# Two transfers change their queue and gain a wait: gate weights on GpSimd's queue, and a hold before the first accumulating transfer

## The chip, the cores and the metric

The kernel runs on one core of a Trainium2 chip. A core has five engines that work side by side and meet at semaphores: TensorE (matrix products, PE in the profile; its weight loads are PEld), VectorE (DVE), ScalarE (ACT), GpSimd (POOL) and SyncE (SP), which here only issues transfers. Sixteen DMA engines carry out the transfers that SP, ScalarE and GpSimd issue; the profile calls SP's queue q1, ScalarE's q10 and GpSimd's q0. The metric is the device time of one execution in microseconds (us).

## The reference

A block of a transformer over 2048 tokens of width 512, in bf16, reduced here to what is computed:

```python
# x: (1, 2048, 512); 32 heads of 16; window of 8 keys, 2 apart
qkv = layernorm(x) @ wqkv
q, k, v = split(qkv)
logits[s, w] = (q[s] . k[s - 2*w]) * 16 ** -0.5      # -1e9 where s - 2*w < 0
o[s] = sum over w of softmax(logits[s])[w] * v[s - 2*w]
h = x + o @ wo
gate, up = layernorm(h) @ W_gate, layernorm(h) @ W_up   # width 1376
out = h + (relu(gate) * up) @ W_down
```

## The kernel before, in words

**Chunks.** The 2048 tokens are handled in four chunks of 512, each in four blocks of 128. For each chunk the kernel normalizes x (`layernorm`), turns the normalized blocks so that the width lies on the partitions, multiplies by the q, k and v weights, and forms the window attention on VectorE: products of q with k shifted by 0 to 14 tokens (L637 in chunk 0, L620 in the others), sums over a head by matmuls with a 0/1 matrix (L628), exponentials, a broadcast of each head's weight over its 16 rows by DMA (L756, eight issues of SP for a chunk), and products with shifted v (L803 in chunk 0, L788 in the others). These products fill a tile `mt` of eight slices of 512 tokens, one tile for each quarter `t` of the width, and the eight slices are added up.

**The sum over eight slices.** In chunks 0, 1 and 2 (`DACC`) the first halving, slices 4 to 7 onto 0 to 3, is done by a DMA of GpSimd's queue that adds to its destination (L831, `f_da`, the steps `ta0` to `ta3`). VectorE does the other two halvings (L791) and the scaling in chunk 0 (L795), which writes the attention's output `OT`, the input of the projection with wo (L867). At the end of chunk 0's attention two tiny copies of GpSimd (L849, L850, the step `lg`) write into the up and down weight tiles; SP's loads of these weights come after them. In the hand-written order GpSimd issues chunk 0's transfers in the order of quarters 1, 3, 2, 0, and VectorE's products and sums follow the same order of quarters.

**Turning the blocks.** Most blocks are turned by TensorE (L531). For some halves of chunks (`DMAT`), both halves of chunk 3's norm of x among them, SP issues a DMA that transposes (L520), one for each block of 128 tokens. All four write one tile `dst`, which is `[128, 4, 512]`; block `j` goes to its columns from `128*j`.

**Setup.** `setup()` issues the first loads. SP loads x of chunk 1, the v weights (L338), x of chunks 2 and 3 (L341), wo (L343) and then the gate weights in two halves (`f_load`, L311). Some loads are held back by a tiny copy of GpSimd: it writes one element of the load's destination and reads one of a tensor that must have arrived first (L334, L337, L339), so that the load, which overwrites the element, has to come after it. The gate weights come without such a copy, behind wo on SP's queue.

**Order.** Every step of the four chunks is an `Op` with an engine, a planned duration, the steps it depends on and buffers. `Plan.order()` runs through them on a model of the engines. The list `RANK` gives each step, by its number, its place among the steps of its engine, so each engine's order is fixed by hand; the model's start times settle in which order the steps of different engines are written out, and which buffer of a set each step takes. The waits themselves come from the data: an instruction waits for the ones that last wrote what it reads. The steps of the four transposes of chunk 3 have the numbers 588, 592, 590 and 594 for blocks 0, 2, 1 and 3 in the order in which SP runs them.

Of the kernel before, what the change touches and what calls it, by code (L numbers as in the profile page):

```python
# [8 lines left out]
P = 128  # L9
BF16 = mybir.dt.bfloat16  # L10
# [82 lines left out]
class Plan:  # L93
# [9 lines left out]
    def add(self, key, *a, **k):  # L103
        op = Op(*a, **k)
        op.key = key
        op.seq = len(self.ops)
        if RANK:
            op.prio = RANK[op.seq]
        self.ops.append(op)
        for b in set(op.take) | set(op.use):  # L110
            b.left += 1
        return op
# [90 lines left out]
def kernel(  # L203
# [11 lines left out]
    nc = tc.nc  # L215
# [32 lines left out]
    sb = ctx.enter_context(tc.tile_pool(name="sb", bufs=1))  # L248
# [9 lines left out]
    same = sb.tile([P, P], BF16, name="same")  # L258
    mask = sb.tile([P, 2, PADL], BF16, name="mask")
    eps_t = sb.tile([P, 1], F32, name="eps_t")  # L260
    warm = sb.tile([P, P], BF16, name="warm")
    ci = sb.tile([P, 1], I32, name="ci")
    tmp = sb.tile([P, 3], I32, name="tmp")
# [4 lines left out]
    wv_sb = sb.tile([P, NT, D], BF16, name="wv_sb")  # L268
# [33 lines left out]
    def f_load(n, i):  # L302
        if n == "d":
            lo, hi = (0, 5) if i == 0 else (5, NFF)
            nc.sync.dma_start(
                wd_sb[:, lo:hi, :], B_W_down[lo * P:hi * P, :].rearrange("(ft p) n -> p ft n", p=P))
            if FTAIL and i:
                nc.sync.dma_start(wd_sb[:FTAIL, NFF, :], B_W_down[NFF * P:F, :])
        else:
            w = (B_W_gate if n == "g" else B_W_up).rearrange("(dt p) f -> p dt f", p=P)  # L310
            nc.sync.dma_start(wgu_sb[:, 2 * i:2 * i + 2, int(n == "u"), :], w[:, 2 * i:2 * i + 2, :])  # L311

    def setup():

        w3_r = A_wqkv.rearrange("(dt p) f -> p dt f", p=P)
        for i in range(2):
            for n, q in enumerate((nc.sync, nc.scalar)):
                j = 2 * i + n
                q.dma_start(x_sm[:, j:j + 1, :], x_rows[:, j:j + 1, :])
                q.dma_start(wqk_sb[:, j:j + 1, :], w3_r[:, j:j + 1, 0:2 * D])  # L320
        nc.scalar.preload_act_table_set("natural_log_exp_and_others")
        V.memset(warm[:], 0.0)  # L322
        make_identity(nc, identity[:])
        nc.gpsimd.memset(eps_t[:], EPS)
        nc.gpsimd.iota(ci[:], pattern=[[0, 1]], base=0, channel_multiplier=1)
        nc.gpsimd.iota(sel_i[:], pattern=[[1, H]], base=0, channel_multiplier=0)
        nc.gpsimd.iota(sp_i[:], pattern=[[1, H], [0, DQ]], base=0, channel_multiplier=0)
        nc.gpsimd.iota(sm_i, pattern=[[0, 4], [1, H]], base=0, channel_multiplier=0)
        nc.gpsimd.iota(mk_i[:], pattern=[[1, PADL]], base=0, channel_multiplier=0)
        nc.gpsimd.memset(kT[:, :, 0:PADL], 0.0)  # L330
        nc.gpsimd.memset(vT[:, :, 0:PADL], 0.0)


        nc.gpsimd.tensor_copy(out=x_sm[0:1, BPC:2 * BPC, 0:1], in_=wqk_sb[0:1, 0, 0:BPC])  # L334
        for j in range(BPC, 2 * BPC):
            nc.sync.dma_start(x_sm[:, j:j + 1, :], x_rows[:, j:j + 1, :])
        nc.gpsimd.tensor_copy(out=wv_sb[0:1, 0, 0:1], in_=wqk_sb[0:1, 3, 0:1])  # L337
        nc.sync.dma_start(wv_sb[:], w3_r[:, :, 2 * D:3 * D])  # L338
        nc.gpsimd.tensor_copy(out=x_sm[0:1, 2 * BPC, 0:1], in_=x_sm[0:1, 2 * BPC - 1, 0:1])  # L339
        for tk in range(2, NCK):  # L340
            nc.sync.dma_start(x_sm[:, tk * BPC:(tk + 1) * BPC, :], x_rows[:, tk * BPC:(tk + 1) * BPC, :])  # L341

        nc.sync.dma_start(wo_sb[:], A_wo.rearrange("(p t) f -> p t f", t=NT))  # L343
        for n in "gud":
            for i in range(2):
                if n not in LATE:
                    f_load(n, i)


        for n, (op, by) in enumerate(((ALU.arith_shift_right, 2), (ALU.bitwise_and, H - 1),  # L350
                                      (ALU.arith_shift_right, 5))):
            V.tensor_scalar(out=tmp[:, n:n + 1], in0=ci[:], scalar1=by, scalar2=None, op0=op)
        V.tensor_copy(out=cf[:, 0:3], in_=tmp[:])
        V.tensor_scalar(out=cf[:, 2:3], in0=cf[:, 2:3], scalar1=1.0 * DIL, scalar2=None, op0=ALU.mult)
        V.tensor_scalar(out=cf[:, 3:4], in0=cf[:, 2:3], scalar1=4.0 * DIL, scalar2=None, op0=ALU.add)
        V.tensor_scalar(out=sel[:], in0=sel_i[:], scalar1=cf[:, 0:1], scalar2=None, op0=ALU.is_equal)
        V.tensor_scalar(out=spread[:], in0=sp_i[:], scalar1=cf[:, 1:2], scalar2=None, op0=ALU.is_equal)
        V.tensor_scalar(out=same[:], in0=sm_i, scalar1=cf[:, 1:2], scalar2=None, op0=ALU.is_equal)
        for hf in range(2):
            V.tensor_scalar(out=mask[:, hf, :], in0=mk_i[:], scalar1=cf[:, 2 + hf:3 + hf],  # L360
                            scalar2=None, op0=ALU.is_ge)
# [11 lines left out]
    PRS, MUH = (0,), (0,)  # L373
    TDD, TDL = 1.3, 1.5
    NWARM, NFILL = 56, (13, 10, 0)
    NHALF = 8
    XT = (3.47, 3.64, 5.45, 5.97, 7.8, 8.2, 8.65, 9.1, 14.8, 16.5)
    WT = (7.75, 7.75, 5.0, 12.5, 18.0, 24.95, 21.4, 28.8)
# [54 lines left out]
    def layernorm(tk, src, dst_slots, pr, groups, on_act, residual=None):  # L433
# [6 lines left out]
        evs = []  # L440
        for grp in groups:
# [72 lines left out]
            for j0 in range(lo, hi, step):  # L514
                if (ln, tk, j0) in DMAT:
                    for j in range(j0, min(j0 + step, hi)):
                        xn, a = norm(j)

                        def f_td(j=j, xn=xn):
                            nc.sync.dma_start_transpose(out=dst.t[:, :, j * P:(j + 1) * P], in_=xn.t[:])  # L520

                        evs.append(add((ln + "td" + gk, tk), "SP", TDD, f_td, [a], pr, take=[dst], use=[xn], lat=0.5, dq=(0.1, 0.64)))
                    continue
                tp, ds, xs = Buf(tp_s), [], []
                for j in range(j0, min(j0 + step, hi)):
                    xn, a = norm(j)

                    def f_tp(j=j, j0=j0, xn=xn, tp=tp):
                        for t in range(NT):
                            o = t * 2 * P + (j - j0) * P  # L530
                            nc.tensor.transpose(tp.t[:].bitcast(BF16)[:, o:o + P],  # L531
                                                xn.t[:, t * P:(t + 1) * P], identity[:])

                    ds.append(add((ln + "tp" + gk, tk), "PE", 4 * TP, f_tp, [a], pr, take=[tp], use=[xn], lat=PEL))
                    if tk == 0 and not residual and j < 2:
                        fill(ds[-1], NFILL[j])
                n = len(ds)

                tev = not residual and tk == 0 and j0 == 1

                def f_ev(j0=j0, n=n, tp=tp, tev=tev):
                    i = tp.t[:].bitcast(BF16).rearrange("p (t c) -> p t c", t=NT)[:, :, 0:n * P]
                    o = dst.t[:, :, j0 * P:(j0 + n) * P]
                    if tev:
                        V.tensor_copy(out=o, in_=i)
                    else:
                        nc.scalar.copy(out=o, in_=i)  # L547

                evs.append(add((ln + ("tv" if tev else "te") + gk, tk), "DVE" if tev else "ACT", 0.36 if tev else (A10 if n == 2 else A5), f_ev, ds, pr, take=[dst], use=[tp], lat=AL))
# [5 lines left out]
    for tk in range(NCK):  # L555
# [224 lines left out]
        for t in range(NT):  # L780
# [46 lines left out]
            for n, du in ((4, D20), (2, D10), (1, D2)):  # L827
                f = lambda n=n, mt=mt, f=f_a: f(n, mt)
                if n == 4 and (tk, t) in DACC:
                    def f_da(mt=mt):  # L830
                        nc.gpsimd.dma_start(mt.t[:, 0:4, :], mt.t[:, 4:8, :], accum_op=ALU.add)  # L831

                    ms = [m] = [add(("ta%d" % t, tk), "POOL", 1.0, f_da, ms, tpr, use=[mt], lat=1.1, dq=(0.75, 2.74))]
                    continue
                if n == 2 and (tk, t) in DAC2:
                    def f_db(mt=mt):
                        nc.gpsimd.dma_start(mt.t[:, 0:2, :], mt.t[:, 2:4, :], accum_op=ALU.add)

                    ms = [m] = [add(("tb%d" % t, tk), "POOL", 0.95, f_db, ms, tpr, use=[mt], lat=1.1, dq=(0.75, 1.37))]
                    continue  # L840
                if n == 1 and tk in EARLY:
                    oev[t] = add(("tree%d" % t, tk), "DVE", du, f_al, ms, tpr, take=[OT], use=[mt], lat=DL)
                else:
                    ms = [m] = [add(("tree%d" % t, tk), "DVE", du, f, ms, tpr, use=[mt], lat=0.11)]
# [232 lines left out]
```

## Time and profile before

| | us |
|---|---|
| median of 3 runs | 194.53 (194.43 to 194.96) |
| the profiled execution | 194.99 |
| its span, first to last instruction | 192.9 |
| TensorE busy in the span | 189.1 |
| VectorE busy | 150.8 |
| ScalarE busy | 115.7 |
| GpSimd busy | 17.3 |

The profile is of one execution; its granted TensorE clock is 1.00 throughout. Its time differs from its span by what lies before the first and after the last instruction. In the page's groups a line such as `L831 POOL DMA_DIRECT2D big<-big x12 | 10.9, 933` names the line of the kernel, the engine, the operation, destination and source by the program's names, the count, the busy time in us and the mean duration in ns. In the order of time a row begins with start and length in us. For DMA issues the length is that of issuing; the time to landing is given apart.

### The profile page before, as it was taken

Reading aid. Unit: us, or ns where it says so; the run is one execution under the profiler, and the core shown is the slowest. Engines: PE = TensorE matmul, PEld = TensorE weight load, DVE = VectorE, ACT = ScalarE, POOL = GpSimd, SP = SyncE. Lnnn points to the kernel's source line nnn. Section 1 sums busy time; section 2 is a strip of 40 time slices with the busy share of each in tenths; the row PEclk is TensorE's granted clock in tenths of the full one; section 3 lists DMA queues with packets and bytes.
Section 4 is the critical chain, followed back from the end, with each engine's and each line's share of the span. In section 5 each row is a group of like instructions: output and inputs, shape, how many; then the busy total and the mean of one; then the engine's idle time right before and its main releaser. Section 6 shows DMA issues by size and latency. Waiting matters only on the chain.

```text
span 192.9 us, 3122 instructions
## 1 busy us (share of the span) xinstructions
PE 189.1 (98%) x1149; PEld 100.5 (52%) x1149; DVE 150.8 (78%) x243; ACT 115.7 (60%) x241; POOL 17.3 (9%) x35
## 2 busy tenths in 40 slices
PE   7999999999999999999999999999999999999994
PEld 7997455555445434644554434444644444464543
DVE  6789999999999999898999979699976534021414
ACT  3479988858897936965265579622647900465500
POOL 3100002311000013100055000003000000000000
PEclk9999999999999999999999999999999999999999
DMA  5789385993914659974269924646001054002033
GB/s 201 240 273 379 104 200 108 198 193 52 370 47 110 123 167 195 189 170 106 43 124 198 195 44 105 169 82 109 3 0 27 1 107 164 30 0 54 0 126 95
DMA packets 25214, 24.61 MB, mean 128 GB/s; under 512 B 11408, under 2 KB 21488, under 8 KB 25200
## 3 DMA queue, kind: packets, MB, share of 16 engines
q1 hardware_dynamic: 22176, 16.26, 30.4%
q0 software_dynamic: 2304, 7.34, 20.6%
q10 hardware_dynamic: 720, 0.82, 1.3%
q8 instruction: 9, 0.15, 0.3%
q14 instruction: 5, 0.04, 0.1%
HBM read 8.42 MB, written 2.10 MB: 55 GB/s over the span
## 4 chain that ended last, share of the span: by engine, by line
PE 98%; DVE 0%; issue 0%
PE bank L940 36%; PE bank L572 22%; PE bank L990 20%; PE bank L867 7%; PE bank L628 4%; PE bank L421 3%; PE bank L907 3%; PE bank L531 2%; PE bank L429 1%; PE bank L713 0%; PE bank L870 0%; DVE row L1003 0%; DVE warm L322 0%
## 5 line engine op out<-in xcount | busy, mean ns | idle before, releaser
L940 PE MATMUL bank<-quad,wgu_sb 128*128 128x512 bf16 x320 | 72.0, 379 | 0.0
L940 PEld LDWEIGHTS <-wgu_sb 128*128 128x128 bf16 x320 | 31.0, 98 | 36.9 <-issue 1.3
L947 ACT ACTIVATE gr<-bank 128x512 bf16<-128x512 f32 x40 | 23.6, 599 | 26.8 <-PE bank L940 24.8
L990 PE MATMUL bank<-wd_sb,gT 128*128 128x512 bf16 (+3 forms) x198 | 39.2, 355 | 0.0
L572 PE MATMUL bank<-quad,wqk_sb 128*128 128x512 bf16 (+1 forms) x160 | 29.8, 336 | 0.1
L990 PEld LDWEIGHTS <-gT 128*128 128x128 bf16 (+1 forms) x198 | 18.4, 98 | 19.4
L620 DVE TENSOR_TENSOR big<-quad,kT 128x4096 bf16<-128x4096 bf16 x12 | 27.2, 2286 | 0.0
L788 DVE TENSOR_TENSOR big<-big,vT 128x4096 bf16<-128x4096 bf16 x12 | 26.9, 2288 | 0.2 <-issue 0.2
L968 DVE TENSOR_TENSOR gT<-gr,up_sb 128x1024 bf16<-128x1024 bf16 x20 | 13.5, 690 | 16.8 <-ACT gr L947 9.9
L944 ACT CAST up_sb<-bank 128x512 bf16<-128x512 f32 x40 | 22.7, 591 | 4.0 <-issue 1.3
L572 PEld LDWEIGHTS <-wqk_sb 128*128 128x128 bf16 x160 | 17.5, 113 | 9.6 <-DMA x_sm<-in_A_x_dram 0.2
L831 POOL DMA_DIRECT2D big<-big x12 | 10.9, 933 | 74.2 <-DVE big L788 45.3
L791 DVE TENSOR_TENSOR big<-big 128x1024 bf16<-128x1024 bf16 (+2 forms) x24 | 16.8, 730 | 0.1
L572 PE MATMUL bank<-quad,wv_sb 128*128 128x512 bf16 x64 | 15.7, 380 | 0.0
L867 PE MATMUL bank<-wo_sb,quad 128*128 128x512 bf16 x64 | 15.1, 379 | 0.0
L547 ACT COPY quad<-bank 128x1024 bf16<-128x1024 bf16 (+1 forms) x10 | 8.6, 889 | 8.5 <-PE bank L531 8.5
L1003 DVE TENSOR_TENSOR row<-x_sm,bank 128x512 bf16<-128x512 bf16 (+2 forms) x10 | 5.6, 582 | 9.8 <-PE bank L990 9.8
L456 ACT ACTIVATE row<-x_sm,mv 128x512 bf16<-128x512 bf16 x12 | 8.6, 717 | 6.8 <-DVE mv L448 6.5
L467 DVE BATCH_NORM_STATS2 st<-x_sm 128x6 f32<-128x512 bf16 x16 | 10.3, 676 | 0.6 <-DMA x_sm<-in_A_x_dram 0.5
L878 DVE SCALAR_TENSOR_TENSOR x_sm<-x_sm,bank 128x512 bf16<-128x512 bf16 x12 | 8.2, 687 | 3.2 <-PE bank L867 3.0
L580 ACT CAST vT<-bank 128x512 bf16<-128x512 f32 x16 | 9.1, 604 | 2.4 <-PE bank L572 2.4
L572 PEld LDWEIGHTS <-wv_sb 128*128 128x128 bf16 x64 | 7.0, 114 | 6.6 <-issue 1.3
(78 smaller groups left out, 175.0 us busy)
## 6 DMA issues: line engine op xcount, KB each, us to landing
big<-big POOLq DMA_DIRECT2D x12, 512.0 KB, 5.8
big<-ex SPq DMA_DIRECT2D x32, 128.0 KB, 2.7
wgu_sb<-in_B_W_gate_dram SPq DMA_DIRECT2D x2, 688.0 KB, 9.1
wgu_sb<-in_B_W_up_dram SPq DMA_DIRECT2D x2, 688.0 KB, 6.1
wd_sb<-in_B_W_down_dram SPq DMA_DIRECT2D x2, 640.0 KB, 4.6
x_sm<-in_A_x_dram SPq DMA_DIRECT2D x2, 512.0 KB, 6.2
x_sm<-up_sb POOLq DMA_DIRECT2D x4, 256.0 KB, 4.5
out_dram<-x_sm SPq DMA_DIRECT2D x4, 256.0 KB, 2.5
```

Source lines behind the costliest of these rows:

```text
L467: V.bn_stats(out=st.t[:], in_=x_sm[:, tk * BPC + j, :])
L572: nc.tensor.matmul(mm.t[:, lo:hi], lhsT=wv_sb[:, dt, t:D:NT] if c == 2 else wqk_sb[:, dt, c * D + t:(c + 1) * D:NT], rhs=xnT.t[:, dt, lo:h ...
L620: V.tensor_tensor(out=pb.t[:].rearrange("p (t w) s -> p t w s", t=2), in0=q4, in1=k4, op=ALU.mult)
L788: V.tensor_tensor(out=mt.t[:], in0=ab.t[:], in1=v8, op=ALU.mult)
L791: V.tensor_tensor(out=mt.t[:, 0:n, :], in0=mt.t[:, 0:n, :], in1=mt.t[:, n:2 * n, :], op=ALU.add)
L831: nc.gpsimd.dma_start(mt.t[:, 0:4, :], mt.t[:, 4:8, :], accum_op=ALU.add)
L867: nc.tensor.matmul(od.t[:], lhsT=OT.t[:, t, j * P:(j + 1) * P], rhs=wo_sb[:, t, :], start=(t == 0), stop=(t == NT - 1 and tk not in RPE))
L940: nc.tensor.matmul(mm.t[:fs, lo:hi], lhsT=wgu_sb[:, dt, g, ft * P: ft * P + fs], rhs=hnT.t[:, dt, lo:hi], start=(dt == 0), stop=(dt == NT ...
L944: nc.scalar.copy(out=ub.t[:fs, i, :], in_=um.t[:fs, :])
L947: nc.scalar.activation(out=gr.t[:fs, i, :], in_=gm.t[:fs, :], func=ACT.Relu)
L968: V.tensor_tensor(out=gt.t[:fs, 0:n, :], in0=gr.t[:fs, 0:n, :], in1=ub.t[:fs, 0:n, :], op=ALU.mult)
L990: nc.tensor.matmul(od.t[:, c0:c1], lhsT=gts[ft].t[:fs, ft % 2, j * P:(j + 1) * P], rhs=wd_sb[:fs, ft, c0:c1], start=(ft == 0), stop=(ft == ...
```

## The change

Two edits. The gate weights' two loads are issued by GpSimd's queue in place of SP's, after a new copy on GpSimd that writes the first element of each gate row group and reads the v weights' tile. And a new copy on GpSimd, ahead of chunk 0's first accumulating transfer, reads one element of block 2 of chunk 3's transposed norm into a new tile `held` that nothing else reads. In the plan all four transfers of chunk 0 get that transpose as a further dependency.

```diff
+    held = sb.tile([P, 1], BF16, name="held")
...
             w = (B_W_gate if n == "g" else B_W_up).rearrange("(dt p) f -> p dt f", p=P)
-            nc.sync.dma_start(wgu_sb[:, 2 * i:2 * i + 2, int(n == "u"), :], w[:, 2 * i:2 * i + 2, :])
+            (nc.gpsimd if n == "g" else nc.sync).dma_start(wgu_sb[:, 2 * i:2 * i + 2, int(n == "u"), :], w[:, 2 * i:2 * i + 2, :])
...
+        nc.gpsimd.tensor_copy(out=wgu_sb[0:1, :, 0, 0:1], in_=wv_sb[0:1, :, 0:1])
         nc.sync.dma_start(wo_sb[:], A_wo.rearrange("(p t) f -> p t f", t=NT))
...
+    HOLD = ("x", 3, 2)
+    holding, turned = [], {}
...
                         evs.append(add((ln + "td" + gk, tk), "SP", TDD, f_td, [a], pr, take=[dst], use=[xn], lat=0.5, dq=(0.1, 0.64)))
+                        if (ln, tk, j) == HOLD:
+                            turned[HOLD] = dst
+                            for h in holding:
+                                h.deps.append(evs[-1])
...
-                    def f_da(mt=mt):
+                    def f_da(mt=mt, tk=tk):
+                        if tk == 0 and HOLD in turned:
+                            nc.gpsimd.tensor_copy(out=held[0:1, 0:1], in_=turned.pop(HOLD).t[0:1, 0, HOLD[2] * P:HOLD[2] * P + 1])
                         nc.gpsimd.dma_start(mt.t[:, 0:4, :], mt.t[:, 4:8, :], accum_op=ALU.add)
...
+                    if tk == 0:
+                        holding.append(m)
```

## The prediction

> **What bounds the kernel now.** I read the page's busy times first, then the chain of work that ended last, in order of time.
>
> ```profile
> span 192.9 us, 3122 instructions
> PE 189.1 (98%) x1149; PEld 100.5 (52%) x1149; DVE 150.8 (78%) x243; ACT 115.7 (60%) x241; POOL 17.3 (9%) x35
> ```
>
> ```profile
> 0.99 6.08 PE bank L421 x56
> ...
> 21.89 0.98 PE bank L628 x16
> ...
> 34.46 13.81 PE bank L572 x64
> 48.27 0.86 PE bank L867 x4
> ...
> 62.68 0.98 PE bank L572 x4
> 63.67 1.73 PE bank L940 x8
> ...
> 190.20 0.02 issue
> ```
>
> The reader is to see that TensorE is never left waiting from 0.99 to 190.20 us: each piece starts where the last ended. 64 matmuls of 512 columns take 13.81 us, 0.216 each, and four take 0.86, so the pieces run at one pace; a few are longer by 0.1 (0.98 at 62.68). Hence two things. A transfer that comes sooner has nothing to win but these crumbs, well under half a microsecond together. And a VectorE step that comes late costs TensorE whatever exceeds the slack at that place, and TensorE has no idle time later in which to get it back. So the question is only whether either edit makes somebody late.
>
> **SP loses two gate loads.** SP in order of time; the columns are start, length, engine, line, operation.
>
> ```profile
> 9.70 0.93 SPq L341 DMA_DIRECT2D x_sm<-in_A_x_dram  x2
> ...
> 11.22 1.76 SPq L311 DMA_DIRECT2D wgu_sb<-in_B_W_gate_dram  x2
> 21.93 5.28 SPq L756 DMA_DIRECT2D big<-ex  x8
> 27.31 5.25 SPq L520 DMA_TRANSPOSE quad<-row  x4
> ```
>
> The two issues occupy SP from 11.22 to 12.98. SP's next work, the broadcasts of chunk 0 (L756), starts at 21.93 because the masked exponentials are done then. Nine idle microseconds lie between: the 1.76 us freed are worth 0.
>
> **GpSimd gains a copy and two loads.**
>
> ```profile
> wv_sb<-in_A_wqkv_dram SPq DMA_DIRECT2D x1, 512.0 KB, 4.1
> 9.50 0.18 POOL L339 COPY x_sm<-x_sm 1x1 bf16<-1x1 bf16 x1 [1.23 <-DMA x_sm<-in_A_x_dram]
> 32.14 1.01 POOL L831 DMA_DIRECT2D big<-big  x1 [22.46 <-DVE row L502]
> 38.72 0.86 POOL L831 DMA_DIRECT2D big<-big  x1 [1.41 <-DVE big L803]
> 45.92 0.70 POOL L850 COPY wd_sb<-big 1x11 bf16<-1x11 bf16 x1
> ```
>
> The v weights are issued at 8.3 and land 4.1 us later, at 12.4. The copy is like the one of L339 (0.18), each load like the issues of L831 (0.86 to 1.01). The first of these was released when its product ended at 31.54 (below) and starts at 32.14, so 0.6 goes from release to issue. Thus 12.4 + 0.2 + 0.6 + 2 x 1.0 = 15.2 us, and GpSimd would have stood idle until 32.1 (22.46 us of idle time in that row): behind the copy that waits for the v weights there are only the two loads and, from 31.5 on, chunk 0's transfers. On GpSimd the cost is 0.
>
> The bytes are the same, on another queue. Three stretches, whose last two columns are the busy share of the DMA engines and GB/s, give the time:
>
> ```profile
> 14.60:21.00 6.40, 6.40 (x63) 4.48 (x62) 6.40 (x7) 6.40 (x12) 0.00 (x0) 1.00 0.86 332
> 21.80:26.00 4.20, 4.20 (x32) 2.07 (x32) 4.20 (x15) 3.27 (x8) 0.00 (x0) 1.00 0.54 122
> 36.00:44.50 8.50, 8.50 (x41) 4.47 (x40) 8.40 (x8) 6.14 (x12) 1.72 (x2) 1.00 1.02 192
> ```
>
> GpSimd's first gate bytes should flow about 1.4 us after its issue at 13.2 (the first accumulating transfer is issued at 32.14, and the engines fill up from about 33.5), at 14.6. From there 6.4 x 332 = 2120 KB are left, 1410 of them gate, 710 of them x and wo; at a full share the pace is 332 / 0.86 = 386 GB/s. They end near 20.5, as before. The lower pace is that of the accumulating transfers, 192 GB/s: 1410 KB take 7.3 us, and with the 710 KB before them at 386 (1.8) the end is 23.7. I take 20.5 to 21.5: plain loads are nearer to the loads of the first row than to additions.
>
> Who needs what, and when:
>
> ```profile
> x_sm<-in_A_x_dram SPq DMA_DIRECT2D x1, 512.0 KB, 6.6
> big<-ex SPq DMA_DIRECT2D x2, 128.0 KB, 2.9
> 21.82 1.28 DVE L467 BATCH_NORM_STATS2 st<-x_sm 128x6 f32<-128x512 bf16 x2
> 27.71 2.36 DVE L803 TENSOR_TENSOR big<-big,vT 128x2048 bf16<-128x2048 bf16 x2
> ```
>
> Chunk 3's x, the second of the two at 9.70, is issued at 10.1 and lands 6.6 later, at 16.7; VectorE reads it first at 21.82, 5.1 us on. Even if gate took the engines first, at the pace of loads, x would be in with 520 KB of wo still to come, 1.4 us ahead of the end: 19 to 20. wo is used at 48.27 and gate at 63.67. The first four broadcasts are issued by 24.0 and land 2.9 later, near 26.9, for a product at 27.71: margin 0.8. With the engines free of gate at 21.5 they are not late, and at 23.7, before the fourth is issued, hardly. Term: 0.
>
> **The hold.** In the hand-written order the four transposes of chunk 3 have ranks 152 (block 0), 161 (block 2), 168 (block 1) and 176 (block 3), so block 2, which the new copy reads, is second on SP.
>
> ```profile
> 28.74 1.21 SPq L520 DMA_TRANSPOSE quad<-row  x1
> DMA to landing us min/median/max: 2.4/2.5/2.7
> 30.32 1.22 DVE L803 TENSOR_TENSOR big<-big,vT 128x2048 bf16<-128x2048 bf16 x1
> 31.34 1.22 SPq L520 DMA_TRANSPOSE quad<-row  x1
> big<-big POOLq DMA_DIRECT2D x1, 512.0 KB, 6.4
> 45.85 0.68 DVE L791 TENSOR_TENSOR big<-big 128x1024 bf16<-128x1024 bf16 x1
> 47.12 0.75 DVE L795 TENSOR_TENSOR quad<-big,rec 128x512 bf16<-128x512 bf16 x2
> ```
>
> The second transpose is issued at 28.74 and lands at 31.1 to 31.4. The copy then takes between 0.18 (as L339) and 0.70 (as L850, eleven elements beside a busy VectorE): it ends between 31.3 and 32.1. The first accumulating transfer can't go before its product ends anyway: 30.32 + 1.22 = 31.54. So the wait hides behind that product and only the copy may show: 0 to 0.6 us, of which I take 0.1, since one element is nearer to L339.
>
> What is queued behind it on GpSimd: the four transfers of chunk 0, then the two copies at 45.66 and 45.92 that release SP's up and down loads. VectorE waits for the four sums. The transfers fill the engines without a pause (share 1.02 from 36 to 44.5), so a late first one makes the last one as late. That one is issued at 38.72, lands 6.4 later at 45.1, and its sum is read at 45.85: slack 0.75. So 0.1 is hidden, and even 0.6. Beyond 0.75 nothing is: the last product ends at 47.87, and TensorE starts the output projection (L867) right at the end of its matmuls (chain, 48.27). From there VectorE's delay is TensorE's.
>
> The planner's times do not move either: the block's planned landing lies ahead of the planned start of the first transfer, as it does in the trace, so order and buffers stay.
>
> **Sum.** SP 0, GpSimd 0, the transfers' new place 0, the hold 0. The profiled execution took 194.99 us, 192.9 in its span and 2.1 around it; the median of the runs shown is 194.53, 0.46 lower. With nothing to add, the forecast is that median: 194.5. A measurement of this kernel can tell about 0.3%, 0.58 us, from no change.
>
> **Rivals.**
>
> *GpSimd and VectorE get in each other's way (slower).* While GpSimd writes the descriptors of the gate loads, from 13.2 to 15.2, VectorE runs the products of L637 without a pause until 21.8, and the score matmuls (L628) start right with their end, so there is no slack at all. If VectorE waited for both issues, 2 x 0.86 = 1.7 us would reach TensorE: 196.2. If instead the descriptors waited for VectorE, gate would flow from 21.8, 1410 KB at 386 GB/s for 3.7 us, into the broadcasts; 1.9 of that fits into idle engine time (from 21.8 to 26 the share is 0.54 of 4.2 us), 1.8 delays them, 0.8 is their margin: 1.0 us, 195.5. It decides once a product of L637 is lengthened, or gate flows past 24. Against it:
>
> ```profile
> L803 DVE TENSOR_TENSOR big<-big,vT 128x2048 bf16<-128x2048 bf16 x8 | 9.4, 1218 | 0.0
> 13.80 8.03 DVE L637 TENSOR_TENSOR big<-quad,kT 128x2048 bf16<-128x2048 bf16 x7
> L637 DVE TENSOR_TENSOR big<-quad,kT 128x2048 bf16<-128x2048 bf16 x8 | 9.2, 1219 | 0.6 <-ACT kT L580 0.6
> ```
>
> The products of L803 run beside four issues of GpSimd, those of L637 beside none, and their means are equal; and the accumulating transfers flowed while VectorE did not pause. The Trainium skill ("SBUF — State Buffer", section "SBUF: two separate sides") speaks for this rival: it says that VectorE and GpSimd share a port pair by an exclusive lock, the loser blocks fully, and loads from GpSimd's queue starve for descriptors. By that rule the time would be in the 195.5 to 196.2 above; the trace, with 1218 against 1219 ns, does not show such a lock.
>
> *The hold lets go late (slower).* If the copy waited for the whole tile, it would be the fourth transpose: issued 31.34, landing at 33.7. Copy and issue start add 0.8: 34.5 in place of 32.14, 2.4 late, less 0.75 of slack: 1.6 us, 196.1. Against it: the product at 27.71 reads one half of its tile while broadcasts into the other half, issued up to 27.2, are still to land. So a wait goes by the part that is read.
>
> *A little faster.* The transposes' data end near 33.3, just ahead of the accumulating ones at 33.5; where the two met in other executions, the hold would spare something. TensorE's crumbs bound it: 194.0 to 194.4.
>
> That the hold holds nothing, as the block lands before the product ends, is my forecast itself.
>
> **Chances.** Covered everywhere, 194.1 to 195.0: 0.76. Port: 0.10. Late hold: 0.06. Faster: 0.08, of which 0.03 beyond 0.3%, which only something that this profile doesn't show could bring. So faster 0.03, same 0.76 + 0.05 = 0.81, slower 0.16. The range goes from 194.0, the low end of the crumbs, to 195.6, just past the port rival's cheaper form.
>
> **What would show it.** Right: gate issues on GpSimd at about 13.2 and 14.1 landing by 22, products of L637 still 1219 ns, the first accumulating transfer issued by 32.8, the output projection at 48.3 in the chain. Wrong: a gap of TensorE at 21.9 (port) or at 48.3 (hold), a longer L637, an accumulating transfer issued after 34. The forecast is wrong if chunk 3's x comes after 21.82, the broadcasts after 27.7, or chunk 0's last sum after 45.85.

## The result, and the profile after

Nineteen executions of the changed kernel took 195.37 us in the median (194.38 to 196.24), nineteen of the kernel before, taken with them, 194.6 (194.2 to 195.35). The ratio is 1.0037, with a 95% interval from 1.0023 to 1.0050: slower by 0.4 to 1.0 us. The forecast was no change.

The profiled execution of the changed kernel took 194.75 us, 192.9 in its span. It is shorter than the one of before (194.99), although the median is longer: it began its real work early. The chain of work that ended last, in order of time (start, length, piece), first of before, then of after:

```profile
8.86 0.60 PE bank L572 x4
...
190.23 0.29 DVE row L1003
```

```profile
8.21 0.60 PE bank L580 x4
...
22.22 6.17 PE bank L580 x28
...
33.81 13.81 PE bank L580 x64
47.63 0.86 PE bank L879 x4
...
63.02 1.73 PE bank L952 x8
...
189.56 0.02 issue
189.58 0.29 DVE row L1015
```

The line numbers have moved by 8 to 12; L580 was L572, L879 was L867, L1015 was L1003. From the first q/k matmul (L580) to VectorE's last addition it is 190.23 - 8.86 = 181.37 us before and 189.58 - 8.21 = 181.37 after. Each piece between stands 0.64 to 0.65 earlier: 33.81 for 34.46, 47.63 for 48.27. In this stretch, which nearly the whole prediction is about, nothing was gained or lost. The 0.64 lies ahead of it. The start of the first q/k matmul differs between executions of one and the same kernel: the three profiled executions of the changed kernel have it at 8.21, 9.26 and 9.33. In the chain of after it goes back to the landing of x at 5.84, in that of before to TensorE's own earlier pieces, most of them warm-up products on the tile `warm` (L421, L429).

GpSimd and VectorE in the changed kernel, in order of time; in brackets the idle time ahead and what ended it:

```profile
13.39 1.04 POOL L344 COPY wgu_sb<-wv_sb 1x4 bf16<-1x4 bf16 x1 [3.65 <-DMA wv_sb<-in_A_wqkv_dram]
14.75 1.66 POOL L312 DMA_DIRECT2D wgu_sb<-in_B_W_gate_dram  x2 [0.32 <-POOL wgu_sb L344]
30.66 0.27 POOL L840 COPY held<-quad 1x1 bf16<-1x1 bf16 x1 [14.25 <-DMA quad<-row]
31.50 0.93 POOL L841 DMA_DIRECT2D big<-big  x1 [0.57 <-DVE row L506]
```

```profile
13.15 8.03 DVE L645 TENSOR_TENSOR big<-quad,kT 128x2048 bf16<-128x2048 bf16 x7
...
21.18 1.28 DVE L471 BATCH_NORM_STATS2 st<-x_sm 128x6 f32<-128x512 bf16 x2
...
27.07 2.36 DVE L811 TENSOR_TENSOR big<-big,vT 128x2048 bf16<-128x2048 bf16 x2
...
43.93 1.96 DVE L799 TENSOR_TENSOR big<-big 128x1024 bf16<-128x1024 bf16 x4
```

The new parts run as described: the copy behind the v weights, two gate loads, the copy into `held`, then the first accumulating transfer at 31.50. That transfer was released by VectorE (DVE), not by the copy: its product (L811) ends at 30.89, the copy at 30.93, and the issue starts 31.497 - 30.892 = 0.61 us behind the product's end, against 32.140 - 31.538 = 0.60 before. VectorE's rows stand 0.64 to 0.65 earlier than before (21.18 for 21.82, 27.07 for 27.71), as does everything.

So where is the time? What grew inside the span lies behind the last addition. The last line of both kernels holds the instructions that close the program: SP checks that all transfers have landed, the engines meet, GpSimd clears the semaphores, the engines meet again. The view of that line gives count, shortest, middle and longest duration in ns, and the first and last start in us. Before, then after:

```profile
L1072 SPq EVENT_SEMAPHORE  x11: 17/28/28, 190.9 to 192.9; - x11
L1072 POOLq EVENT_SEMAPHORE  x4: 17/17/17, 192.2 to 192.8; - x4
L1072 POOLq DRAIN  x2: 40/66/93, 192.4 to 192.7; - x2
L1072 POOLq EVENT_SEMAPHORE_RANGE_CLEAR  x1: 139/139/139, 192.5 to 192.5; - x1
```

```profile
L1084 SPq EVENT_SEMAPHORE  x11: 17/28/28, 190.3 to 192.9; - x11
L1084 POOLq EVENT_SEMAPHORE  x4: 17/17/17, 191.7 to 192.8; - x4
L1084 POOLq DRAIN  x2: 93/140/187, 191.9 to 192.5; - x2
L1084 POOLq EVENT_SEMAPHORE_RANGE_CLEAR  x1: 139/139/139, 192.0 to 192.0; - x1
```

The reader is to see two things. GpSimd's four semaphore instructions stretch over 0.6 us before (192.2 to 192.8) and 1.1 after (191.7 to 192.8): between the clearing and the second DRAIN there is 0.2 before and 0.5 after. And from the last addition to GpSimd's first of these instructions (GpSimd's release) it is 192.23 - 190.23 = 2.00 before and 191.70 - 189.58 = 2.12 after (starts to the hundredth, from the trace).

The execution's own time less the start of the last addition is 194.99 - 190.23 = 4.76 us before and 194.75 - 189.58 = 5.17 after: 0.41 more. This "whole end" counts all the time outside the span as if it lay behind it; the profile does not show how much of that lies ahead of the first instruction.

### The profile page after: what moved, and what is told of

It reads as the page before. It is cut to its first block, busy times and chain, and to the rows that moved or that the text cites. A ratio compares the mean times of both kernels' runs of the same rounds, so it can differ in the third digit from the quotient of the medians.

```text
span 192.9 us, 3125 instructions
## 1 busy us (share of the span) xinstructions
PE 188.1 (98%) x1149; PEld 99.2 (51%) x1149; DVE 150.6 (78%) x243; ACT 115.9 (60%) x241; POOL 20.1 (10%) x39
## 4 chain that ended last, share of the span: by engine, by line
PE 94%; DMA 2%; DVE 1%; issue 0%; SPq 0%; ACT 0%
PE bank L952 36%; PE bank L580 22%; PE bank L1002 20%; PE bank L879 7%; PE bank L636 4%; PE bank L919 3%; DMA x_sm<-in_A_x_dram 2%; PE bank L539 2%; PE bank L882 0%; PE bank L721 0%; DVE st L471 0%; SPq L321 0%; SPq L320 0%; DVE row L506 0%; ACT rs L484 0%
## 5 line engine op out<-in xcount | busy, mean ns | idle before, releaser
L580 PE MATMUL bank<-quad,wqk_sb 128*128 128x512 bf16 (+1 forms) x160 | 29.8, 336 | 0.3 <-ACT rs L484 0.3
L580 PEld LDWEIGHTS <-wqk_sb 128*128 128x128 bf16 x160 | 17.5, 113 | 9.9 <-issue 0.5
L580 PE MATMUL bank<-quad,wv_sb 128*128 128x512 bf16 x64 | 15.7, 380 | 0.0
L879 PE MATMUL bank<-wo_sb,quad 128*128 128x512 bf16 x64 | 15.1, 379 | 0.0
L1015 DVE TENSOR_TENSOR row<-x_sm,bank 128x512 bf16<-128x512 bf16 (+2 forms) x10 | 5.6, 581 | 9.8 <-PE bank L1002 9.8
L580 PEld LDWEIGHTS <-wv_sb 128*128 128x128 bf16 x64 | 7.0, 114 | 6.6 <-issue 1.3
```

What stands on the lines that cost most here:

```text
L580: nc.tensor.matmul(mm.t[:, lo:hi], lhsT=wv_sb[:, dt, t:D:NT] if c == 2 else wqk_sb[:, dt, c * D + t:(c + 1) * D:NT], rhs=xnT.t[:, dt, lo:h ...
L879: nc.tensor.matmul(od.t[:], lhsT=OT.t[:, t, j * P:(j + 1) * P], rhs=wo_sb[:, t, :], start=(t == 0), stop=(t == NT - 1 and tk not in RPE))
```

## The experiments

The twelve experiments come in three groups of four, and the kernel before was run beside each group (35, 35 and 34 executions). At first the theories were about the stretch that the prediction is about: the moved gate bytes are late into the broadcasts (G), the hold is late (H), or both (B).

**1. The gate loads alone.**

```diff
-    HOLD = ("x", 3, 2)
+    HOLD = None
```

> The first edit alone: gate weights on GpSimd's queue behind the copy that waits for the v weights, no hold. Theory G (the gate loads, whose bytes now flow until 22 to 23.5 us, reach into the first broadcasts and delay them now and then): 0.4 to 0.8 us slower than before, ratio 1.002 to 1.004, like the whole change. Theory H (the hold lets the first accumulating transfer go late, because its copy is kept waiting beside VectorE): no difference, within 0.2 us. Theory B (it takes both: the gate loads make the transposes late and only the hold passes that on): no difference, within 0.2 us.

Measured: 194.96 us against 194.84, ratio 1.0003 [0.9982, 1.0025].

**2. The hold alone.**

```diff
-            (nc.gpsimd if n == "g" else nc.sync).dma_start(wgu_sb[:, 2 * i:2 * i + 2, int(n == "u"), :], w[:, 2 * i:2 * i + 2, :])
+            nc.sync.dma_start(wgu_sb[:, 2 * i:2 * i + 2, int(n == "u"), :], w[:, 2 * i:2 * i + 2, :])
...
-        nc.gpsimd.tensor_copy(out=wgu_sb[0:1, :, 0, 0:1], in_=wv_sb[0:1, :, 0:1])
```

> The second edit alone: the hold, with the gate weights on SP as before. Theory H: 0.5 to 1 us slower than before, and in the trace an accumulating transfer of chunk 0 issued well over 0.6 us after its product's end. Theory G: no difference, within 0.2 us. Theory B: no difference, within 0.2 us.

Measured: 194.81 against 194.84, ratio 0.9992 [0.9977, 1.0007].

**3. The change once more**, with no edit, beside the others.

> The change as it is, on the chip that times the others of this call, and for the trace of a second execution. All theories: 0.5 to 1 us slower than before. If the traced execution is one of the longer ones (a span over 193.4 us), theory G expects TensorE's gap near 28 to 31 us after late broadcasts, theory H near 48 us after a late last sum.

Measured: 195.71 against 194.84, ratio 1.0023 [1.0004, 1.0042]. The slowing is there again.

**4. The gate loads on SP's queue, behind the new copy; no hold.**

```diff
-            (nc.gpsimd if n == "g" else nc.sync).dma_start(wgu_sb[:, 2 * i:2 * i + 2, int(n == "u"), :], w[:, 2 * i:2 * i + 2, :])
+            nc.sync.dma_start(wgu_sb[:, 2 * i:2 * i + 2, int(n == "u"), :], w[:, 2 * i:2 * i + 2, :])
...
-    HOLD = ("x", 3, 2)
+    HOLD = None
```

> Gate weights on SP's queue as before, but behind the copy that waits for the v weights; no hold. It parts the later start from the other queue. Theory G by lateness: 0.3 to 0.8 us slower than before, as the bytes end later on any queue. Theory G by the queue (GpSimd's descriptors are written slowly, or its bytes crowd out SP's): no difference, within 0.2 us. Theories H and B: no difference, within 0.2 us.

Measured: 195.09 against 194.84, ratio 1.0020 [0.9994, 1.0045]. One of the twelve executions, which was not profiled, took 197.25.

The medians of these four tell little apart; the traces tell more. For the gate loads alone, the first q/k matmul in the chain of work, and VectorE's last row in order of time:

```profile
8.61 0.60 PE bank L580 x4
```

```profile
189.98 0.29 DVE L1015 TENSOR_TENSOR row<-x_sm,bank 128x128 bf16<-128x128 bf16 x1 [0.33 <-PE bank L1002]
```

The same two rows for the hold alone:

```profile
8.81 0.60 PE bank L579 x4
```

```profile
190.18 0.29 DVE L1014 TENSOR_TENSOR row<-x_sm,bank 128x128 bf16<-128x128 bf16 x1 [0.33 <-PE bank L1001]
```

And for the change once more:

```profile
9.26 0.60 PE bank L580 x4
```

```profile
190.62 0.29 DVE L1015 TENSOR_TENSOR row<-x_sm,bank 128x128 bf16<-128x128 bf16 x1 [0.33 <-PE bank L1002]
```

189.98 - 8.61 and 190.18 - 8.81 are both 181.37, and 190.62 - 9.26 is 181.36. Experiment 4 has 181.37 too. With G, H or B this stretch would have grown in some of them. The execution profiled in 3 was one of the long ones (195.76, against a median of 195.71), and its stretch is no longer than the others. So all three theories fell, as far as the profiled executions go.

What did differ was the closing of the program: with the gate loads on GpSimd it was long, with them on SP it was short. The second group asked why. Theory I: it is GpSimd's instruction stream. The kernel before has 66 instructions on GpSimd, the change 71 (two copies, two loads, one wait more; semaphore instructions and DRAINs are counted, which the page's x35 leaves out), and in each kernel that has so many, the 69th starts 0.36 to 0.38 us late. Theory Q: it is the two further transfers of GpSimd's queue. Theory C: executions that are not profiled lose time in the body.

**5. The kernel before, with four idle GpSimd instructions more** (70), and no transfer moved.

```diff
+    pad = sb.tile([P, 4], F32, name="pad")
...
+        for i in range(4):
+            nc.gpsimd.memset(pad[:, i:i + 1], 0.0)
```

> The kernel before with four tiny memsets of a tile that nothing reads, on GpSimd in its idle time after 2.4 us; no transfer moves and nothing waits. Theory I (the first runs: TensorE's stretch is the same 181.35 us in every trace, and what the change adds lies behind the last store, where GpSimd's 69th instruction starts 0.35 us late; its program before has 66, and the change has 71): 70 instructions here, so 0.25 to 0.45 us slower than before, and in the trace the end sequence from GpSimd's release to the last instruction takes 1.1 us in place of 0.66. Theory Q (the end is longer because two more transfers went through GpSimd's queue): no difference, 0.66 us at the end. Theory C (the change costs in the body, in executions that were not traced): no difference.

Measured: 195.06 against 194.64, ratio 1.0024 [1.0007, 1.0041]. Four tiny instructions, done within the first 3 us and awaited by nobody, and the kernel is measured slower, though its whole end is only 0.12 us longer (4.88), which does not account for all of that. Its closing:

```profile
L1075 POOLq EVENT_SEMAPHORE  x4: 17/17/17, 191.7 to 192.7; - x4
L1075 POOLq DRAIN  x2: 40/71/102, 191.8 to 192.1; - x2
```

The four semaphore instructions stretch over 1.0 us. Both DRAINs are in time here, and the late one is the instruction behind them: that is the 69th of this kernel, as the second DRAIN is of the change. Theory I was right about the span; Q is not needed, for here no transfer was moved.

**6. The change, with three memsets moved from GpSimd to VectorE** (68).

```diff
-        nc.gpsimd.memset(eps_t[:], EPS)
...
-        nc.gpsimd.memset(kT[:, :, 0:PADL], 0.0)
-        nc.gpsimd.memset(vT[:, :, 0:PADL], 0.0)
...
+        V.memset(eps_t[:], EPS)
+        V.memset(kT[:, :, 0:PADL], 0.0)
+        V.memset(vT[:, :, 0:PADL], 0.0)
```

> The change with three small memsets (eps_t and the zero columns of kT and vT) moved from GpSimd to VectorE, so that GpSimd's program has 68 instructions in place of 71. Theory I: within 0.2 us of before, and the end sequence takes 0.66 us again. Theory Q: the end sequence stays at 1.1 us and the time 0.3 us or more above before. Theory C: 0.4 to 0.9 us slower than before, like the change, with a short or a long end.

Measured: 195.09 against 194.64, ratio 1.0025 [1.0007, 1.0044].

```profile
L1084 POOLq EVENT_SEMAPHORE  x4: 17/17/17, 191.4 to 192.0; - x4
L1084 POOLq DRAIN  x2: 46/70/93, 191.6 to 191.8; - x2
```

The closing in the span is short again (0.6), as Theory I says, although both gate loads are still on GpSimd's queue: Q fell. But the time is not back: what lies outside the span grew, from 2.02 us in the mean of before to 2.28. So Theory I held for the span and not for the whole time, and the two parts must be read together.

**7. The change a third time.**

> The change once more on the chip that times the others of this call. Theory I: 0.25 to 0.45 us slower than before, the same as the kernel with four memsets, within 0.2 us of it. Theory C: 0.5 to 0.9 us slower, clearly above the kernel with four memsets. An end sequence of 1.1 us with the 69th instruction late, and TensorE's stretch at 181.35 us, by theories I and Q.

Measured: 195.15 against 194.64, ratio 1.0020 [0.9999, 1.0040]; the interval just reaches 1.

**8. The kernel before, with two idle GpSimd instructions more** (68).

```diff
+    pad = sb.tile([P, 2], F32, name="pad")
...
+        for i in range(2):
+            nc.gpsimd.memset(pad[:, i:i + 1], 0.0)
```

> The kernel before with two tiny memsets on GpSimd: 68 instructions. Theory I: within 0.2 us of before, and the end sequence takes 0.66 us, since no 69th instruction is there. If each added instruction cost something by itself, the end or the opening would be 0.1 to 0.2 us longer.

Measured: 194.91 against 194.64, ratio 1.0003 [0.9983, 1.0023]. The closing in the span is short, the time outside it 2.27 us in the mean, as in the sixth.

Beside GpSimd's part there is SP's. SP checks the transfers' semaphores one behind the other, at least 0.06 us each. The records of before and after around the check that waits for the last store (start in us, engine, instruction, what it awaits):

```
before  191.639 Sync EVENT_SEMAPHORE  S[107], S[111]
before  192.004 Sync EVENT_SEMAPHORE  S[108], S[101]   <- the last store, issued with semaphore 108
before  192.066 Sync EVENT_SEMAPHORE  S[109], S[110]
before  192.131 Sync DRAIN

after   191.355 Sync EVENT_SEMAPHORE  S[106], S[112]   <- the last store, issued with semaphore 106
after   191.416 Sync EVENT_SEMAPHORE  S[107], S[111]
after   191.476 Sync EVENT_SEMAPHORE  S[108], S[101]
after   191.537 Sync EVENT_SEMAPHORE  S[109], S[110]
after   191.602 Sync DRAIN
```

SP takes its transfers' semaphores in turn. With two transfers fewer on SP the last store gets the one two places earlier, and two checks more follow behind it: 0.12 us.

The third group put these two counts back one by one. Theory L: the change pays at the end, for GpSimd's instructions and SP's checks. Theory S: only the random start differs. Theory T: the moved transfers cost executions that are not profiled.

**9. The kernel before, with five GpSimd instructions fewer** (61).

```diff
-    sel_i, sp_i, mk_i = ints[:, 0:H], ints[:, H:H + P], ints[:, H + P:H + P + PADL]
-    sm_i = ints[:, 512:512 + P]
+    sp_i, sm_i = ints[:, H:H + P], ints[:, 512:512 + P]
+    sel_i, mk_i = sm_i[:, 0:H], sm_i[:, 0:PADL]
...
-        nc.gpsimd.memset(eps_t[:], EPS)
-        nc.gpsimd.iota(sel_i[:], pattern=[[1, H]], base=0, channel_multiplier=0)
-        nc.gpsimd.iota(mk_i[:], pattern=[[1, PADL]], base=0, channel_multiplier=0)
-        nc.gpsimd.memset(kT[:, :, 0:PADL], 0.0)
-        nc.gpsimd.memset(vT[:, :, 0:PADL], 0.0)
...
+        V.memset(eps_t[:], EPS)
+        V.memset(kT[:, :, 0:PADL], 0.0)
+        V.memset(vT[:, :, 0:PADL], 0.0)
```

> The kernel before with GpSimd's program five instructions shorter (61 instead of 66): the three memsets of eps_t, kT and vT go to VectorE, the index rows of sel_i and mk_i are read from sm_i instead of being made by iotas of their own. All the rest as before. Theory L (the change pays at the end of the program: for the length of GpSimd's program, and for SP's list of last checks): from 66 to 68 instructions the stretch from GpSimd's release to the end plus the time outside the span grew by 0.26 us, 0.05 to 0.13 per instruction; if that goes on below 66, the time is 0.1 to 0.45 us under the kernel before, with the stretch inside the span still 0.72 and the time outside it under 2.0. Theory S (the end does not matter; kernels differ only by when the first q/k matmul starts, at random): the same as before within 0.15 us.

Measured: 195.10 against 194.69, ratio 1.0015 [0.9991, 1.0039]. The gain that L hoped for did not come: 2.06 us outside the span, as with 66. Five instructions fewer than 66 win nothing.

**10. The change, with wo loaded in three parts**, so that SP has as many transfers as before.

```diff
-        nc.sync.dma_start(wo_sb[:], A_wo.rearrange("(p t) f -> p t f", t=NT))
+        for lo, hi in ((0, 2), (2, 3), (3, 4)):
+            nc.sync.dma_start(wo_sb[:, lo:hi, :], A_wo.rearrange("(p t) f -> p t f", t=NT)[:, lo:hi, :])
```

> The change, with the load of wo cut into three, so that SP issues two DMAs more, as many as in the kernel before, and the semaphore of the last store stands where it stood there in the order of SP's last checks. GpSimd's program keeps its 71 instructions. Theory L: from VectorE's last addition to GpSimd's release 2.00 us instead of the change's 2.12; GpSimd's end still 1.23 with its late 69th instruction; time less the start of the first q/k matmul 186.4 instead of 186.5; in all 0.1 us less than the change, so 0.25 to 0.45 above before. Theory S: before within 0.15 us, or wherever the starts fall. Theory T (the two loads on GpSimd's queue cost executions that are not profiled): as the change, 0.4 to 0.7 above before.

Measured: 195.37 against 194.69, ratio 1.0020 [0.9995, 1.0045]. From the last addition to GpSimd's release 191.985 - 189.984 = 2.00 in place of 2.12, and the long closing of the change. In the time, 0.68 above before in the medians, T's 0.4 to 0.7 fits better than L's 0.25 to 0.45; the interval holds both.

```profile
L1085 POOLq EVENT_SEMAPHORE  x4: 17/17/17, 192.0 to 193.1; - x4
L1085 POOLq DRAIN  x2: 93/140/187, 192.1 to 192.8; - x2
```

**11. The change with both counts put back**: GpSimd at 66 by the edits of the ninth, wo in three parts as in the tenth. Gate loads, copy and hold all stay.

```diff
-    sel_i, sp_i, mk_i = ints[:, 0:H], ints[:, H:H + P], ints[:, H + P:H + P + PADL]
-    sm_i = ints[:, 512:512 + P]
+    sp_i, sm_i = ints[:, H:H + P], ints[:, 512:512 + P]
+    sel_i, mk_i = sm_i[:, 0:H], sm_i[:, 0:PADL]
...
+        for lo, hi in ((0, 2), (2, 3), (3, 4)):
+            nc.sync.dma_start(wo_sb[:, lo:hi, :], A_wo.rearrange("(p t) f -> p t f", t=NT)[:, lo:hi, :])
```

> The change with both counts put back: five instructions of GpSimd left out as in the first kernel of this call (66, as many as the kernel before), and wo in three loads (as many SP DMAs as before). Gate loads on GpSimd's queue, the copy ahead of them and the hold all stay. Theory L: the release 2.00 us behind VectorE's last addition, GpSimd's end 0.72, no late 69th instruction, 2.0 outside the span; time less the start of the first q/k matmul 186.1 to 186.2, and the time that of the kernel before within 0.2 us. Theory T (moved loads or hold cost untraced executions): 0.4 to 0.7 above before. Theory S: wherever the starts fall, with no tie to the two counts.

Measured: 195.06 against 194.69, ratio 1.0011 [0.9986, 1.0036]. First q/k matmul, last addition, closing:

```profile
9.49 0.60 PE bank L579 x4
```

```profile
190.85 0.29 DVE L1014 TENSOR_TENSOR row<-x_sm,bank 128x128 bf16<-128x128 bf16 x1 [0.33 <-PE bank L1001]
```

```profile
L1083 POOLq EVENT_SEMAPHORE  x4: 17/17/17, 192.9 to 193.5; - x4
L1083 POOLq DRAIN  x2: 46/70/93, 193.0 to 193.3; - x2
L1083 POOLq EVENT_SEMAPHORE_RANGE_CLEAR  x1: 139/139/139, 193.1 to 193.1; - x1
```

The profiled execution took 195.62 us, so from the last addition to its end 195.62 - 190.85 = 4.77 us, against 4.76 before and 5.17 in the change. This is what L forecast of the end: the closing 0.72, the release 2.00 behind the addition, 2.04 outside the span. Both edits are in this kernel, and its end is that of the kernel before. Of the time L forecast more than came: it was to be within 0.2 us of before, and the median is 0.37 above, with an interval that holds both that and nothing.

**12. The ninth, with wo in two parts**, so that the last store has the very last check.

```diff
-        nc.sync.dma_start(wo_sb[:], A_wo.rearrange("(p t) f -> p t f", t=NT))
+        for lo, hi in ((0, 2), (2, 4)):
+            nc.sync.dma_start(wo_sb[:, lo:hi, :], A_wo.rearrange("(p t) f -> p t f", t=NT)[:, lo:hi, :])
```

> The first kernel of this call (before, GpSimd at 61 instructions) with wo cut into two loads, so that the last store's semaphore is the very last of SP's checks instead of the last but one. Theory L: the release about 0.06 us sooner behind VectorE's last addition than in that kernel (1.94 instead of 2.00), the time 0.05 to 0.1 below it, so 0.15 to 0.5 under the kernel before: this would be the fastest of all. Theory S: before within 0.15 us.

Measured: 194.87 against 194.69, ratio 1.0000 [0.9974, 1.0026]. The release comes 1.95 us behind the last addition, 0.05 sooner than in kernel 9, where one check follows that of the last store; no gain in the time can be told. No kernel of this study beats the kernel before.

All the ends together, each from its one profiled execution (us; "whole end" is the execution's time less the start of the last addition):

| kernel | GpSimd instructions | addition to GpSimd's release | release to end of span | outside the span | whole end |
|---|---|---|---|---|---|
| 9 | 61 | 2.00 | 0.73 | 2.06 | 4.79 |
| 12 | 61 | 1.95 | 0.73 | 2.06 | 4.75 |
| before | 66 | 2.00 | 0.72 | 2.05 | 4.76 |
| 11 | 66 | 2.00 | 0.72 | 2.04 | 4.77 |
| 2 | 67 | 2.00 | 0.72 | 2.12 | 4.84 |
| 8 | 68 | 2.00 | 0.72 | 2.29 | 5.00 |
| 4 | 68 | 2.00 | 0.72 | 2.27 | 4.99 |
| 6 | 68 | 2.11 | 0.73 | 2.27 | 5.11 |
| 5 | 70 | 2.00 | 1.11 | 1.76 | 4.88 |
| 1 | 70 | 2.12 | 1.12 | 1.79 | 5.03 |
| 10 | 71 | 2.00 | 1.23 | 1.78 | 5.01 |
| change (after, 3, 7) | 71 | 2.12 | 1.23 | 1.78 to 1.81 | 5.13 to 5.17 |

The third column follows SP's transfers alone: 2.11 to 2.12 in the kernels with the gate loads taken from SP and not made up for, 1.95 to 2.00 in the others. The fourth and fifth follow GpSimd's count alone: together 2.8 at 61 to 67, 3.0 at 68, 2.9 at 70 and 3.0 at 71. In these kernels the number of instructions decides, and it does not matter what they are: idle memsets (8) and a copy with a wait (4) give the same.

**How much of the slowing this is.** The three measurements of the change hold 42 executions with a mean of 195.30 us; 123 executions of the kernel before have 194.74. The difference is 0.56, with a standard error of 0.09. The whole end accounts for about 0.4 (5.13 to 5.17 against 4.76). The rest, 0.15, is under twice its error.

That the end counts in the time shows when all executions are put together by the whole end of their kernel:

| whole end, us | kernels | executions | mean time, us | standard error |
|---|---|---|---|---|
| 4.75 to 4.79 | before, 9, 11, 12 | 159 | 194.78 | 0.04 |
| 4.84 to 4.88 | 2, 5 | 24 | 194.88 | 0.07 |
| 4.99 to 5.03 | 1, 4, 8, 10 | 45 | 195.08 | 0.09 |
| 5.11 to 5.17 | 6 and the change | 54 | 195.27 | 0.07 |

Single kernels scatter more: kernel 11, with the end of before, is 0.31 us above it in the mean, with a standard error of 0.17, and kernel 8, with an end 0.24 longer, is level with it. So the total of kernel 11, 1.0011 with an interval from 0.9986 to 1.0036, can't tell 0.1 from 0.4; it is its end that shows the return.

In the traces the other thing that differs, but for one stretch of kernel 12 (below), is when the first q/k matmul starts, from 7.84 (kernel 8) to 9.49 (kernel 11), in kernels with the gate loads moved and in kernels without. Most executions have their span on record; less the 181.37 and the kernel's own piece of span behind the last addition it gives an estimate of that start, 8.79 in the mean of the change (42) and 8.66 in that of before (104), with a standard error of 0.09 on the difference. Whether the changed kernel starts a tenth later on average, or loses it in the body of executions without a profile (theories C and T), is left open: these executions can't tell it.

## Why the prediction was wrong

Its bounds held the time (195.37 within 194.0 to 195.6), by luck, since the upper one came from the port rival, which did not come about; its forecast, the same within 0.3%, did not come about either. By its own steps:

- **TensorE never waits, so only lateness counts.** Right from the first q/k matmul on: 181.36 to 181.37 us to the last addition in thirteen of fourteen traces. Not right from 0.99: the pieces ahead of that matmul are mostly warm-up products, and its start moves by up to 1.65 us. In the fourteenth trace (kernel 12) the stretch is 182.32, because the v weights of that execution landed late, 6.78 us after their issue, and the chain of its work starts from them; that kernel moves no gate load:

```profile
7.65 6.78 DMA wv_sb<-in_A_wqkv_dram
```

- **SP loses two gate loads, worth 0.** This term was mis-sized. In the body it is 0. At the end it costs 0.12 us, since the last store's check moves two places forward in SP's list; kernel 10 gives two transfers back and has 2.00 for 2.12.
- **GpSimd gains a copy and two loads, cost 0.** This term was mis-sized too, and it is the larger one: five instructions more cost 0.51 us inside the span (1.23 for 0.72) and bring 0.24 to 0.27 back outside it. Kernel 5 has a long closing too (1.11) without any of the change.
- **The sum.** "192.9 in its span and 2.1 around it ... With nothing to add, the forecast is that median": here is the step that failed. The 4.76 us of the whole end, 2.7 in the span and 2.05 outside it, were carried over as a constant, without asking what they are made of; they became 5.13 to 5.17, by 0.12 for SP's checks and by 0.25 to 0.28 for GpSimd's five instructions. The chain of waits stood there with its last piece at 190.20 and a span of 192.9; the 2.7 between them were not read.
- **The transfers' new place, 0.** Right. The v weights landed 5.6 us after their issue, not 4.1, and the copy took longer, so the gate loads were issued at 14.75 and 15.6, not 13.2 and 14.1; the first bytes were wanted at 63.02 all the same. Their landing, 7.3 us after issue in the mean:

```profile
wgu_sb<-in_B_W_gate_dram POOLq DMA_DIRECT2D x2, 688.0 KB, 7.3
x_sm<-in_A_x_dram SPq DMA_DIRECT2D x2, 512.0 KB, 6.5
wv_sb<-in_A_wqkv_dram SPq DMA_DIRECT2D x1, 512.0 KB, 5.6
L645 DVE TENSOR_TENSOR big<-quad,kT 128x2048 bf16<-128x2048 bf16 x8 | 9.2, 1222 | 0.5 <-ACT kT L588 0.5
```

- They landed at 21.6 and 23.3 (6.8 and 7.7 behind their issues; 19.8 and 21.5 in the kernel before), so their end is later than "20.5 to 21.5" and just inside the bound of 23.7. VectorE read chunk 3's x and the broadcasts at their usual distance.
- **The hold, 0.** Right in the body; its copy is one of the five instructions above. It took 0.27 (bounds 0.18 to 0.70) and was done at 30.93, 0.04 behind the end of the product, within the 0.60 that lies between that end and the issue anyway, so nothing of it shows. With the hold alone, the time is that of before (0.9992).
- **The port rival** did not come about in VectorE's time: L645 at 1222 ns for 1219, with both gate issues beside it. Yet the other half of its rule is to be seen. The new copy (L344) took 1.04 us in the changed kernel, 13.39 to 14.43, beside a product of L645 that runs from 13.15 to 14.38, and 0.85 in kernel 1, where the product ends at 13.56 and the copy at 13.62; in kernels 3, 7, 10 and 11, where it began ahead of the first product, 0.19 to 0.20. So GpSimd's copy did wait for VectorE, as the Trainium skill has it ("SBUF — State Buffer", section "SBUF: two separate sides"), while the issuing of the two gate loads, beside the products too, took 1.65 to 1.66 us in all of these kernels, and in the changed kernel 1.3 of their 1.4 MB had flowed by 21.0, while these products ran to 21.18. The same section of the Trainium skill states the starving of GpSimd's transfers for VectorE operations in a 2-port mode, and the lock of an operation with two inputs only against GpSimd operations that read SBUF; the prediction took it more widely.
- **The late hold** did not come about: the copy started at 30.66, with the second transpose, and the transfer waited neither for the fourth nor for the copy.
- **Chances.** 0.16 for slower came from those two rivals alone. The mechanism that decided was not among the cases.

## What to carry to other kernels

When a kernel's body is covered and the question is a few tenths of a microsecond, the closing of the program belongs to the sum: compare the chain's last piece with the span's end and the span with the execution's time, and read the closing line's rows of SP and GpSimd. Instructions that an edit adds to GpSimd can lengthen it, however well they are hidden, though not in proportion (68 here end later than 70), and a transfer taken from SP's list changes how many checks come behind that of the last store. And one profiled execution against another tells nothing about such a difference until both are counted from a common event, here the first q/k matmul.

## What the runs showed of the hardware that was not expected

- GpSimd's 69th instruction starts 0.36 to 0.38 us late, in all six traces of kernels that have one, whatever it is: the second DRAIN in the change (1.23 for the closing), the semaphore instruction behind it in kernels 1 and 5 (1.11 to 1.12). With 68 instructions no instruction of the closing is late, but the time outside the span is 2.27 to 2.29 in place of 2.05. What makes that place late was not tried further.
- What lies outside the span is not a constant of the chip: 2.04 to 2.06 us with 61 and 66 GpSimd instructions, 2.12 with 67, 2.27 to 2.29 with 68, 1.76 to 1.81 with 70 and 71.
- A copy of four elements on GpSimd takes 0.19 to 0.20 us when it begins ahead of VectorE's first product of 128 x 2048 elements, and 0.85 and 1.04 us when it begins inside one: it then ends 0.06 us behind that product. The issuing of a transfer beside such products takes 0.76 to 0.90 us, no more than the 0.83 to 0.93 of this kernel's other issues.
- The first q/k matmul starts anywhere from 7.84 to 9.49 us, more than the whole effect of this change.
